# Fused attention, expert routing and two feed-forward layers: eight weight tiles are no longer decoded in the attention, and the decoder and the second route are laid out anew

## The chip, the cores and the metric

The kernel runs on one core of a Trainium2 chip. The metric is the device time of one execution in microseconds, the median of several runs. The engines are named as in the profile: PE (TensorE, matmuls; PEld its weight loads), DVE (VectorE), ACT (ScalarE), POOL (GpSimd), SP (SyncE, which here only issues DMAs).

## The reference

Three layers follow each other. The attention has no softmax: per head `kv = k^T v`, `out = q kv`, and each row of 64 is normalised by its root mean square. The 4608 tokens of width 512 are then routed to 8 experts with a greedy rule over all sorted logits, at most 576 tokens per expert, and each expert is a two-layer network with ReLU. The last layer takes the maximum of three products and one more product.

```
x      = norm(q @ (k.T @ v)) * g_norm                  # 8 batches x 576 tokens, 8 heads of 64
logits = x @ w_gate                                    # 4608 x 8
for idx in argsort(-logits.flatten()):                 # greedy
    tok, e = divmod(idx, 8)
    if assigned[tok] < 0 and counts[e] < 576: assigned[tok] = e
y[e]   = relu(x[e] @ w1[e]) @ w2[e]                    # 512 -> 1024 -> 512, per expert
out    = max(y @ v1, y @ v2, y @ v3) @ w_out           # 512 -> 768 -> 512
```

The four matrices of the last layer are 64-bit floats; all others are 32-bit.

## The kernel before, in words

**Attention** (the loop over `bp`, lines 437 to 488). Four passes of two batches each. A pass computes the K-V products (`kv`, line 189), copies them to SBUF on ScalarE (`kv_out`, 194 and 195), transposes them (`bd_t`, 200), multiplies in the gate weights (`bd_w`, 207), and then makes nine output tiles (`o_tile`, 225): ScalarE squares and copies each tile (230, 234), VectorE sums the squares (235), `norm_b` makes the norms and logits, and SP stores the rows (`y_store`, 271). K, V and Q of the next passes are loaded on SP (`load`), Q in two parts, the second ("r") when the tiles of the pass are done.

**Decoding.** The last layer's weights are 24 tiles of 128 x 512 numbers (0 to 17 of the three first matrices, 18 to 23 of the last). Each is loaded as 128 x 1024 32-bit words (`load64`, 355) and turned into an fp32 value and its split into two fp32r parts, in four steps: `dec_a`, two operations of ScalarE (367, 368); `dec_b`, a shift and a combination on VectorE (373, 375) and an addition on GpSimd (377); `dec_c`, a rounding copy on ScalarE (383, 385); `dec_d`, a subtraction (391, 394) on GpSimd for tiles 0 to 3 and 18 to 23, else on VectorE. Tiles 18 to 23 are stored to DRAM (395) and their buffers take tiles 12 to 17, which are loaded by `more64`. `TILES` says which tiles are decoded inside the attention, `ORDER` the sequence of the rest, and `decoder` is a generator that does one tile in two pieces.

**Threshold rounds** (`top_search`, 538). The first expert's threshold is found in seven rounds: VectorE compares all keys with up to 63 thresholds (573), TensorE counts (575), `narrow` compares the counts (542), TensorE spreads the result (545), VectorE sums it (548). Each round waits for the one before. `narrow` also begins a tile of the decoder (`begin`).

**Experts** (the loop over `p`, line 941). For each expert TensorE does both products of the expert and the last layer in groups of twelve matmuls (`mm3`, 880 to 882): three fp32r products for each fp32 one. After each group `tick` (906) runs one piece of the decoder and one step of `route`, the generator `phase(p + 1)` that finds the next expert's tokens. A route picks each token's best expert (`pick`, `keys`), transposes the masked keys on TensorE (708, 714, 717), and searches the threshold in 11 and 5 steps (`search`): two sign passes with a sum on ScalarE (506), a comparison on VectorE (508), a product (512), a matmul (515) and four small operations (519 to 526). Every `yield` is a tick between what stands before it and what stands behind. The rows of the next expert are then gathered (`gather`, 854), scaled (860) and transposed (869).

The order on each engine is the order of the program's text; a `yield` is what sets on which tick a step is issued. The lines that matter most:

```
    TILES = ((), (), (0, 1, 2, 3), (4, 5, 6, 7), ())
    ORDER = [8, 18, 9, 19, 10, 20, 11, 21, 22, 23] + list(range(12, 18))
        beat += 1
        bg_piece(1)
        if route is not None and beat > 6:
                next(route)
```

## Time and profile before

| what | value |
|---|---|
| median of 3 runs | 1289.95 us (1289.1 to 1290.58) |
| the profiled execution | 1291.93 us, its span 1290.2 us |
| busy share of the span: PE, PEld, DVE, ACT, POOL | 94%, 89%, 50%, 37%, 31% |
| the chain that ended last | PE 71%, DVE 13%, DMA 6%, ACT 5%, issue 3% |
| mean granted clock | 0.970 |
| HBM read and written | 111.43 MB, 23.20 MB |

The profile is of one execution. Busy time counts the time in which an engine has an instruction; a granted clock of 1.00 is 2.4 GHz, and an engine's idle time costs something only where the chain that ended last goes through it. The chain goes through the attention's loads to about 97 us, through the threshold rounds from 130 to 148, and then nearly always through TensorE.

### The profile page before, as it was taken

The numbers are of one execution on the slowest core, as the hardware profiler recorded it, in microseconds if no ns is written. First come the engines' busy times: TensorE is split into PE (matmuls) and PEld (weight loads), VectorE is DVE, ScalarE is ACT, GpSimd is POOL, SyncE is SP. The second block draws the span as 40 slices with busy tenths as digits, with TensorE's granted clock in tenths as the row PEclk, the third lists the DMA queues.
The fourth block names the chain that finished last, engine by engine and source line by source line (L and its number), as shares of the span: only waits on it lengthen the run. The fifth ranks groups of instructions, "written<-read, shape, count | busy, mean of one in ns | idle before, by whom it ended". The sixth has DMA issues, their size and how long they took to land.

```text
span 1290.2 us, 23274 instructions
## 1 busy us (share of the span) xinstructions
PE 1216.6 (94%) x8878; PEld 1142.4 (89%) x8880; DVE 645.4 (50%) x2075; ACT 480.8 (37%) x1166; POOL 401.9 (31%) x483
## 2 busy tenths in 40 slices
PE   9987687798999999999999999999999999999997
PEld 7876477798899989998999999998999899989995
DVE  2659779763576336652766157725763331122110
ACT  3557336641363225422552155314531331133110
POOL 0013025313531344134412452244313561154121
PEclk9979688899999999999999999999999999999998
DMA  9996534403230313121321133112302153013101
GB/s 337 403 362 230 199 96 162 156 1 102 90 101 18 104 42 110 63 84 45 107 75 58 48 114 99 58 47 95 105 28 83 58 157 103 1 57 115 66 1 41
DMA packets 52033, 136.15 MB, mean 106 GB/s; under 512 B 5840, under 2 KB 10448, under 8 KB 50384
## 3 DMA queue, kind: packets, MB, share of 16 engines
q1 hardware_dynamic: 44672, 110.25, 25.3%
q0 software_dynamic: 6944, 24.38, 5.6%
q8 instruction: 70, 1.15, 0.4%
q14 instruction: 43, 0.35, 0.1%
q10 hardware_dynamic: 304, 0.02, 0.0%
HBM read 111.43 MB, written 23.20 MB: 104 GB/s over the span
## 4 chain that ended last, share of the span: by engine, by line
PE 71%; DVE 13%; DMA 6%; ACT 5%; issue 3%; POOL 1%; SPq 1%; POOLq 0%; ACTq 0%; DVEq 0%
PE mm L880 18%; PE mm L882 17%; PE mm L881 17%; PE mm L1037 4%; PE mm L1039 4%; PE mm L1038 4%; ACT W L506 3%; DVE T L526 2%; DMA w<-w_dram 2%; PE kv L189 2%; DMA vta<-vx_dram 2%; PE tp L869 1%; DVE H L970 1%; PE o L225 1%; DMA xd<-y 1%
## 5 line engine op out<-in xcount | busy, mean ns | idle before, releaser
L880 PE MATMUL mm<-X,w 128*128 128x288 f32 x1152 | 345.7, 300 | 0.0
L882 PE MATMUL mm<-X,w 128*128 128x288 f32 x1152 | 340.3, 295 | 0.0
L881 PE MATMUL mm<-X,w 128*128 128x288 f32 x1152 | 340.3, 295 | 0.0
L880 PEld LDWEIGHTS mm<-X,w 128*128 128x128 f32 x1152 | 217.8, 189 | 0.4
L881 PEld LDWEIGHTS mm<-X,w 128*128 128x128 f32 x1152 | 217.4, 189 | 0.0
L882 PEld LDWEIGHTS mm<-X,w 128*128 128x128 f32 x1152 | 217.2, 189 | 0.0
L1012 POOL TENSOR_TENSOR H<-t,H 128x288 fp32r<-128x288 f32 x96 | 79.3, 826 | 432.7 <-ACT H L1011 432.7
L829 POOL TENSOR_TENSOR ring<-raw,ring 128x512 fp32r<-128x512 f32 x112 | 144.5, 1293 | 215.3 <-ACT ring L820 201.6
L1010 DVE TENSOR_TENSOR t<-mm,t 128x288 f32<-128x288 f32 x192 | 87.0, 453 | 164.7 <-PE mm L882 164.0
L880 PE MATMUL mm<-X,ring 128*128 128x288 f32 (+1 forms) x512 | 155.8, 304 | 1.6 <-ACT X L875 1.6
L880 PE MATMUL mm<-H,ring 128*128 128x288 f32 x512 | 156.0, 305 | 0.0
L882 PE MATMUL mm<-X,ring 128*128 128x288 f32 (+1 forms) x512 | 152.7, 298 | 0.3 <-DVE X L876 0.3
L881 PE MATMUL mm<-X,ring 128*128 128x288 f32 (+1 forms) x512 | 152.3, 298 | 0.0
L881 PE MATMUL mm<-H,ring 128*128 128x288 f32 x512 | 151.8, 296 | 0.0
L882 PE MATMUL mm<-H,ring 128*128 128x288 f32 x512 | 151.7, 296 | 0.0
L506 ACT ACTIVATE W<-KT,T 96x384 bf16<-96x384 f32 x168 | 102.1, 608 | 109.4 <-DVE T L526 109.4
L1011 ACT CAST H<-t 128x288 fp32r<-128x288 f32 x96 | 41.3, 430 | 262.9 <-DVE t L1010 262.9
L880 PEld LDWEIGHTS mm<-X,ring 128*128 128x128 f32 x512 | 98.2, 192 | 2.3 <-ACT X L875 2.3
L882 PEld LDWEIGHTS mm<-X,ring 128*128 128x128 f32 x512 | 97.6, 191 | 0.9 <-DVE X L876 0.9
L880 PEld LDWEIGHTS mm<-H,ring 128*128 128x128 f32 x512 | 97.4, 190 | 0.8 <-issue 0.8
L881 PEld LDWEIGHTS mm<-X,ring 128*128 128x128 f32 x512 | 97.8, 191 | 0.0
L881 PEld LDWEIGHTS mm<-H,ring 128*128 128x128 f32 x512 | 97.0, 190 | 0.0
(257 smaller groups left out, 2052.9 us busy)
## 6 DMA issues: line engine op xcount, KB each, us to landing
raw<-w_dram SPq DMA_DIRECT2D x128, 256.0 KB, 2.7
ring<-wod SPq DMA_DIRECT2D x48, 512.0 KB, 3.5
xd<-y SPq DMA_DIRECT2D x36, 288.0 KB, 8.5
w<-w_dram SPq DMA_DIRECT2D x18, 512.0 KB, 9.3
qta<-qx_dram SPq DMA_DIRECT2D x4, 1280.0 KB, 13.3
qtb<-qx_dram SPq DMA_DIRECT2D x4, 1024.0 KB, 11.1
kta<-kx_dram SPq DMA_DIRECT2D x3, 1280.0 KB, 17.5
vta<-vx_dram SPq DMA_DIRECT2D x3, 1280.0 KB, 16.6
```

The lines of the kernel that those rows point to most:

```text
L189: nc.tensor.matmul(KV[b][:, hp, :], KT[bp, o][p0:p1, c - o * CA, h], VT[bp, o][p0:p1, c - o * CA, h], start=(i == 0), stop=(i == len(cs) - 1))
L506: nc.scalar.activation(gs[:, j], KT, AF.Sign, bias=T[0:96, 1 + j:2 + j], scale=-1.0, accum_out=cnt[:, j:j + 1])
L829: (nc.gpsimd if stream[m][0] else nc.vector).tensor_sub(t[:, 1], raw, t[:, 0])
L880: nc.tensor.matmul(ps, wt[:, 0, ws], x[:, 0, xs], start=first, stop=False)
L881: nc.tensor.matmul(ps, wt[:, 1, ws], x[:, 0, xs], start=False, stop=False)
L882: nc.tensor.matmul(ps, wt[:, 0, ws], x[:, 1, xs], start=False, stop=last)
L1010: nc.vector.tensor_tensor(t2, ps[:, :HS], (t1, t1, t2)[j], op=OP.max)
L1011: nc.scalar.copy(m[:, 0, cs], t2)
L1012: nc.gpsimd.tensor_sub(m[:, 1, cs], t2, m[:, 0, cs])
L1037: nc.tensor.matmul(pss[c], l[:, 0, ls], w[:, 0, :], start=(fc == 0), stop=False)
L1038: nc.tensor.matmul(pss[c], l[:, 0, ls], w[:, 1, :], start=False, stop=False)
L1039: nc.tensor.matmul(pss[c], l[:, 1, ls], w[:, 0, :], start=False, stop=(fc == 5))
```

## The change

No tile is decoded in the attention (`TILES` is empty). Tiles 0 to 7 are loaded at the end of the third pass, behind the last load of Q, and the ten that were loaded at the end of the attention still are. `ORDER` begins with tiles 0 to 7. In the threshold rounds `narrow` begins two tiles, no longer one, and five of the rounds issue the shift of one tile on VectorE (`dec_x`), ahead of the comparison of the counts. In the expert loop the second route takes a step on every tick from the first, and the decoder a piece on every tick from the fifth. The routes have one more tick ahead of each transpose of masked keys (which the route of expert 1 had already), and the first eight search steps of expert 1's route have one more tick ahead of their matmul. A buffer for the shift's result is saved; `late` is replaced by the count of tiles that are ready.

```diff
--- before.py
+++ after.py
@@ -367,13 +367,16 @@
         nc.scalar.activation(up, up, AF.Copy, scale=2.0 ** -112)
         nc.scalar.activation(lo, lo.bitcast(U32), AF.Copy, scale=2.0 ** -29)
 
+    def dec_x(i):
+        XV[i] = w3a.tile([128, NH // 2 * XW], I32, name="dv", tag="xg", bufs=6)[:, 0:DM]
+        nc.vector.tensor_scalar(XV[i], words(i)[1], 3, None, op0=OP.logical_shift_left)
+
     def dec_b(i):
         r, up = words(i)
-        x = w3a.tile([128, DM], I32, name="dx", bufs=1)
-        nc.vector.tensor_scalar(x, up, 3, None, op0=OP.logical_shift_left)
-        yield
-        nc.vector.scalar_tensor_tensor(up, up, -2 ** 31, x, op0=OP.bitwise_and, op1=OP.bitwise_or)
-        XV[i] = w3a.tile([128, NH // 2 * XW], I32, name="dv", tag="xg", bufs=6)[:, 0:DM]
+        if i not in XV:
+            dec_x(i)
+        yield
+        nc.vector.scalar_tensor_tensor(up, up, -2 ** 31, XV[i], op0=OP.bitwise_and, op1=OP.bitwise_or)
         nc.gpsimd.tensor_tensor(XV[i], up, r, op=OP.add)
 
     def dec_c(i):
@@ -395,7 +398,7 @@
             nc.gpsimd.dma_start(wod[(i - 18) * 128:(i - 17) * 128], w.bitcast(F32).rearrange("p (j n) -> p j n", j=2))
             late64.append(i - 6)
 
-    ORDER = [8, 18, 9, 19, 10, 20, 11, 21, 22, 23] + list(range(12, 18))
+    ORDER = [0, 1, 2, 3, 4, 5, 6, 7, 8, 18, 9, 19, 10, 20, 11, 21, 22, 23] + list(range(12, 18))
     ND = len(ORDER)
     ready, late64, begun = [], [], []
 
@@ -433,7 +436,7 @@
             for _ in st_(i) or ():
                 pass
 
-    TILES = ((), (), (0, 1, 2, 3), (4, 5, 6, 7), ())
+    TILES = ((), (), (), (), ())
     for bp in range(NP):
         b0, b1, t0 = 2 * bp, 2 * bp + 1, bp * TP
         new = TILES[bp]
@@ -478,10 +481,13 @@
             y_store()
         if bp + 1 < NP:
             load(bp + 1, "r")
-        else:
+        if bp == NP - 2:
+            for i in range(0, NA):
+                load64(i)
+        if bp + 1 == NP:
             lds.close()
             w3p = ctx.enter_context(tc.tile_pool(name="w3p", bufs=1, side="right"))
-            for i in ORDER[:10]:
+            for i in ORDER[8:18]:
                 load64(i)
         norm_b()
         y_store()
@@ -495,7 +501,7 @@
     def bc(ap):
         return ap[:, :, None].to_broadcast([128, E, NT])
 
-    def search(KT, i0, i1, REM2):
+    def search(KT, i0, i1, REM2, slow):
 
         T = SC[:, i0]
         for i in range(i0, i1):
@@ -511,6 +517,8 @@
             ce = rt.tile([96, 3, E], BF, name="ce")
             nc.vector.tensor_mul(ce, BM, cnt[:, :, None].to_broadcast([96, 3, E]))
             yield
+            if slow and i < 8:
+                yield
             pc = rps.tile([128, 512], F32, name="rps")
             nc.tensor.matmul(pc[:, :3 * E], ones[0:96], ce.rearrange("p j e -> p (j e)"), start=True, stop=True)
             ex = rt.tile([128, 3, E], F32, name="ex")
@@ -538,9 +546,11 @@
     def top_search(g2):
 
         def narrow(pc, J, i, K):
+            if 2 <= len(begun) <= 10:
+                dec_x(ORDER[len(begun) // 2 - 1])
             ex = rt.tile([E, 64], BF, name="ex8")
             nc.vector.tensor_scalar(ex[:, 0:J], pc[0:E, 0:J], float(CAPN), None, op0=OP.is_gt)
-            begin(1)
+            begin(2)
             pb = rps.tile([128, 512], F32, name="rps")
             nc.tensor.matmul(pb[:, 0:J], ones8, ex[:, 0:J], start=True, stop=True)
             sc = rt.tile([128, 64], BF, name="scr")
@@ -707,8 +717,7 @@
                     gs = slice(12 * g, 12 * g + 12)
                     nc.vector.tensor_mul(K[:, g], oh[:, :, gs], key[:, None, gs].to_broadcast([128, E, 12]))
                 yield
-                if p == 1:
-                    yield
+                yield
                 pt = rps.tile([128, 512], F32, name="rps")
                 for g in range(3):
                     nc.tensor.transpose(pt[0:96, g * 128:g * 128 + 128], K[:, g].rearrange("p e c -> p (e c)"),
@@ -717,7 +726,7 @@
                 nc.scalar.copy(KT[i], pt[0:96, 0:384])
                 yield
             b1 = None
-            for r in search(KT[0], 0, 11, REM2):
+            for r in search(KT[0], 0, 11, REM2, p == 1):
                 if r is None:
                     yield
                 else:
@@ -734,7 +743,7 @@
             nc.vector.tensor_add(sf, sf, t)
             yield
             b2 = None
-            for r in search(KT[0], 11, 16, REM2):
+            for r in search(KT[0], 11, 16, REM2, False):
                 if r is None:
                     yield
                 else:
@@ -842,7 +851,6 @@
     X = xp.tile([128, 4, 2, S], F32R, name="X")
     LO = xp.tile([128, 6, 2, 128], F32R, name="LO")
     XG = {}
-    late = False
 
     def gather(p):
         for c in range(5):
@@ -906,13 +914,14 @@
     def tick():
         nonlocal route, beat
         beat += 1
-        bg_piece(1)
-        if route is not None and beat > 6:
+        if beat > 4:
+            bg_piece(1)
+        if route is not None:
             try:
                 next(route)
             except StopIteration:
                 route = None
-                if late:
+                if len(ready) == 24:
                     gather(len(XG) // 5)
 
     def drain():
@@ -1013,8 +1022,6 @@
             o = 64 * (p % 2)
             nc.gpsimd.tensor_copy(LO[:, fc, :, o:o + 64], m[:, :, 512:576].bitcast(F32))
         drain()
-        if p == 0:
-            late = True
         if (p + 1, 0) not in XG and p + 1 < E:
             gather(p + 1)
         if p + 1 < E:
```

Three places where the order of instructions moves. ScalarE, third pass of the attention, between the end of the second pass (L252) and the transposes' copy (L202); `w_0` and `w_1` are tiles 0 and 1:

```order
 L234 COPY y<-o 128x576
 L252 ACTIVATE t<-a 128x24
-L367 ACTIVATE w_0_549<-w_0_549 128x512
-L368 ACTIVATE w_0_549<-w_0_549 128x512
 L194 COPY BD_227<-kv 64x4x64
 L195 COPY BD_227<-kv 64x4x64
-L367 ACTIVATE w_1_551<-w_1_551 128x512
-L368 ACTIVATE w_1_551<-w_1_551 128x512
 L202 COPY bdt<-bt 128x512
 L208 COPY BD_227<-bt 128x4x16
```

The copies of the K-V product now follow the second pass directly; the first steps of tiles 0 and 1 are gone from there, and so are those of the other six.

VectorE, first threshold round (`W` is the comparison with the thresholds, `ex` that of the counts, `scr` the sum), before:

```order
L573 SCALAR_TENSOR_TENSOR W_1377<-H_232,ns,TH 128x372
L573 SCALAR_TENSOR_TENSOR W_1391<-H_232,ns,TH 128x372
L578 TENSOR_SCALAR H_232<-H_232,ns 128x36
L542 TENSOR_SCALAR ex_1406<-rps 8x31
L548 SCALAR_TENSOR_TENSOR scr,ns<-rps,SV 128x31
```

and of the change:

```order
L583 SCALAR_TENSOR_TENSOR W_1303<-H_232,ns,TH 128x372
L583 SCALAR_TENSOR_TENSOR W_1317<-H_232,ns,TH 128x372
L588 TENSOR_SCALAR H_232<-H_232,ns 128x36
L372 TENSOR_SCALAR dv<-w_0_947 128x512
L552 TENSOR_SCALAR ex_1334<-rps 8x31
L558 SCALAR_TENSOR_TENSOR scr,ns<-rps,SV 128x31
```

The shift of tile 0 stands between the subtraction and the comparison that waits for TensorE's counts; the next four rounds have the same.

SP, expert 0, behind the last weight loads of the first expert (`w_14` to `w_17` are the tiles loaded into freed buffers, `ring<-wod` the reads of the stored tiles 18 to 23), before:

```order
L355 DMA w_14_2385<-w_dram 128x1024
L355 DMA w_15_2501<-w_dram 128x1024
L355 DMA w_16_2563<-w_dram 128x1024
L817 DMA ring<-wod 128x1024
L355 DMA w_17_2619<-w_dram 128x1024
L817 DMA ring<-wod 128x1024 x3
```

and of the change:

```order
L355 DMA w_14_2967<-w_dram 128x1024
L355 DMA w_15_3019<-w_dram 128x1024
L355 DMA w_16_3080<-w_dram 128x1024
L355 DMA w_17_3135<-w_dram 128x1024
L826 DMA ring<-wod 128x1024 x4
```

The first read of the stored tiles now stands behind the last of the six loads.

## Rows read from the trace of the kernel before

**Rows 1.** Windows: us, busy (count) per engine, clock, DMA share, GB/s.

```profile
57.00:75.00 18.00, 12.79 (x98) 10.98 (x97) 10.45 (x38) 5.65 (x12) 0.62 (x3) 0.90 1.01 410
75.00:97.00 22.00, 20.77 (x136) 19.12 (x137) 12.57 (x25) 15.53 (x33) 4.60 (x5) 0.77 0.95 341
...
478.00:612.00 134.00, 132.50 (x976) 126.55 (x975) 73.71 (x258) 53.22 (x141) 48.03 (x55) 1.00 0.24 76
```

**Rows 2.** Timeline of the third pass: start, us, instruction [idle before <-releaser].

```profile
74.10 0.65 ACT L367 ACTIVATE w<-w 128x512 f32<-128x512 f32 x1 [9.59 <-DMA w<-w_dram]
...
75.99 1.12 PE L200 MATMUL bt<-ident,BD 128*128 128x128 f32 x4 [5.96 <-ACT BD L195]
...
76.69 0.55 SPq L107 DMA_DIRECT2D qtb<-qx_dram  x1
```

**Rows 3.** Windows of expert 0, engines PE, PEld, DVE, ACT, POOL.

```profile
175.00:190.00 15.00, 13.82 (x101) 13.47 (x101) 11.53 (x26) 6.64 (x15) 3.12 (x3) 1.00 0.20 54
190.00:240.00 50.00, 40.19 (x267) 38.78 (x266) 47.95 (x117) 32.32 (x75) 24.12 (x23) 0.90 0.48 164
240.00:264.00 24.00, 18.34 (x117) 17.54 (x116) 14.68 (x54) 11.48 (x32) 2.88 (x3) 0.86 0.24 89
264.00:312.00 48.00, 48.00 (x393) 46.96 (x392) 29.39 (x119) 14.46 (x41) 9.86 (x16) 1.00 0.12 39
```

**Rows 4.** Groups by line, 170 to 339 us: busy, mean ns | idle before, releaser.

```profile
L377 POOL TENSOR_TENSOR dv<-w 128x512 int32<-128x512 int32 x16 | 17.5, 1092 | 51.6 <-DVE w L375 26.8 <-DVE ce L512 8.8 <-ACT w L385 7.4
...
L375 DVE SCALAR_TENSOR_TENSOR w<-w,dx 128x512 int32<-128x512 int32 x16 | 12.0, 751 | 0.0
...
L373 DVE TENSOR_SCALAR dx<-w 128x512 int32<-128x512 int32 x16 | 9.7, 608 | 0.1
...
L391 DVE TENSOR_TENSOR w<-dv,w 128x512 fp32r<-128x512 f32 x10 | 8.2, 825 | 4.8 <-ACT w L383 4.7
...
L367 ACT ACTIVATE w<-w 128x512 f32<-128x512 f32 x9 | 6.1, 679 | 6.7 <-DMA w<-w_dram 6.7
```

**Rows 5.** Timeline of ScalarE: what it evacuates after ticks 13 and 38.

```profile
197.67 0.41 ACT L967 ACTIVATE H<-mm 128x288 fp32r<-128x288 f32 x1 [1.19 <-PE mm L882]
...
264.04 0.39 ACT L1007 COPY t<-mm 128x288 f32<-128x288 f32 x1
```

**Rows 6.** The chain that ended last: start, us, the fourth pass's transposes.

```profile
105.34 0.44 PE bt L200 x4
```

**Rows 7.** Timeline of ScalarE: last square of pass three with its copy, of pass four.

```profile
97.02 0.60 ACT L230 ACTIVATE sq<-o 128x512 f32<-128x512 f32 x1 [0.25 <-PE o L225]
97.52 0.63 ACT L234 COPY y<-o 128x576 f32<-128x576 f32 x1
...
122.75 0.60 ACT L230 ACTIVATE sq<-o 128x512 f32<-128x512 f32 x1 [0.47 <-PE o L225]
```

**Rows 8.** DMA issues, 76.5 to 77.5 us: count, KB each, us to landing.

```profile
qtb<-qx_dram SPq DMA_DIRECT2D x1, 1024.0 KB, 9.0
```

**Rows 9.** Timeline ahead of expert 0: gathers on GpSimd, the four subtractions on VectorE.

```profile
161.77 2.49 DVE L391 TENSOR_TENSOR w<-dv,w 128x512 fp32r<-128x512 f32 x4
...
162.58 1.32 POOL L854 DMA_INDIRECT xg<-xd,idx  x1 [0.31 <-issue]
164.20 0.95 POOL L854 DMA_INDIRECT xg<-xd,idx  x1 [0.30 <-issue]
```

**Rows 10.** Timeline of VectorE: a shift in the third pass, a comparison in the rounds.

```profile
74.79 0.43 DVE L373 TENSOR_SCALAR dx<-w 128x512 int32<-128x512 int32 x1 [5.80 <-ACT w L367]
...
133.58 0.18 DVE L542 TENSOR_SCALAR ex<-rps 8x31 bf16<-8x31 f32 x1 [0.29 <-PE rps L575]
```

**Rows 11.** Waits, whole span: us in total, times, longest.

```profile
ACT W L636 <- DVE q L634: 16.4, 2, 15.8
```

**Rows 12.** Waits of the key transposes: whole span, then 170 to 339 us.

```profile
PE rps L714 <- DVE V L708: 11.6, 6, 4.6
...
PE rps L714 <- DVE V L708: 4.6, 1, 4.6
```

## The prediction

> **What bounds the kernel now.** I read the chain that ended last first: TensorE holds most of it, so a change pays only where TensorE waits or runs slowly. The windows by stage then say where that is. In an expert of the steady state (478 to 612 us) TensorE is busy for 132.5 of 134 us at clock 1.00 [rows 1]: nothing to gain there but the 1.5 us. Two stages are not like that.
>
> The attention's third pass. ScalarE meets the first step of tile 0 at 64.5 us and stands 9.59 us until the tile's DMA has landed, at 74.1 [rows 2]. Behind it in ScalarE's queue stands the copy of the K-V product, and TensorE's transposes wait for that copy 5.96 us, to 75.99 [rows 2]. TensorE then runs at a mean clock of 0.77 for the next 22 us [rows 1], part of it at the lower of its two levels (1.2 GHz), which it entered with this hole. The DMA share is 1.01 and 0.95 in these two windows [rows 1]: the queues are full, the tiles are part of that load.
>
> Expert 0. VectorE is busy for 47.95 of the 50 us from 190 to 240, while TensorE is busy 40.19 at clock 0.90 [rows 3]; from 264 to 312 TensorE is continuous and VectorE busy 29.39 of 48 [rows 3]. So here VectorE is the bound for the first half and idle for much of the second. What ends the waits is the decoder and the second route at once on VectorE, and, at 240 to 264, ScalarE waiting for tiles that are loaded a second time: 6.7 us on DMA [rows 4].
>
> **Part by part.** A tick is one group of twelve matmuls and what is issued behind it; expert 0 has 67 of them, and the last 29 (264.04 to 312) take 48 us, 1.65 us each [rows 3, 5].
>
> *A, attention: no tile decoded, eight loads behind the last Q load.* The hole of 5.96 us goes, since ScalarE's copy no longer has a load ahead of it. The clock is worth a second term: from the transposes to the last square the third pass takes 75.99 to 97.02, 21.0 us, the fourth 105.34 to 122.75, 17.4 us [rows 2, 6, 7]; the difference, 3.6, is what a pass without the hole should not pay. Together 9.6; the fourth pass also loses its four first steps on ScalarE and the shifts on VectorE, some of which delay it. I take **-10**. What is late next is data: the second half of Q for this pass is issued at 76.69 and lands 9.0 us later, at 85.7 [rows 2, 8]. Four tiles of 0.524 MB ahead of it, at the 410 GB/s of that stage [rows 1], are 5.1 us, so it lands near 80.6. Without the hole the transposes start at 70.0. The last square follows 17.4 us later, at 87.4, and the four tiles that read this half cost ScalarE a square and a copy each, 0.60 + 0.63 us [rows 7], some 5 us: the half is wanted near 82.4, and just there. If data is the bound after all, the gain is those 5.1 us. Ends: -5 and -12. SP's queue is moved past nothing that is waited for: the eight loads stand behind the last Q load, and the stores of y behind them are first read by the gathers after 160 us [rows 9].
>
> *B, threshold rounds: 28 first-step operations on ScalarE, five shifts on VectorE.* ScalarE does 14 of them there now and then stands 15.8 us until VectorE's one-hot is made [rows 11]; fourteen more of 0.68 us [rows 4] are 9.5 us and fit. They cost nothing; without that cover a tile would cost its 1.4 us. The shifts stand ahead of a comparison before which VectorE is idle 0.29 us [rows 10], waiting for TensorE. A shift with GpSimd idle took 0.43 us [rows 10]. Five times 0.14 is 0.7, some of it covered by the shifts' overlap with the operation ahead: **+0.5**. Ends: 0, and five times 0.608 less 0.29, the mean of a shift in expert 0 [rows 4], where GpSimd works too: +1.6.
>
> *C, four subtractions leave VectorE before expert 0.* They run from 161.77 to 164.26; the gather that GpSimd writes beside them takes 1.32 us, a later one 0.95 [rows 9]. The scalings wait for gathers, so **-0.4**, ends 0 and -1. The Trainium skill (SBUF — State Buffer, section "Who interferes with whom") infers that a two-input VectorE operation does not hold up GpSimd's descriptor writing; by that sentence C would be 0. The rows speak for a little, and I follow them.
>
> *D, expert 0.* To VectorE's work come eight tiles of shift and combine, 8 x (0.608 + 0.751) = 10.9 us, less five shifts already done, 3.0, plus four subtractions of tiles 4 to 7, 4 x 0.825 = 3.3 [rows 4]: +11.1 on 103.6 us of busy time between 175 and 312 [rows 3], so 114.7. These operations' means include what GpSimd's extra adds cost. The idle time of VectorE there is now 33.4 us: 3.5 in the first window, 2.0, 9.3 and 18.6 [rows 3]. The route begins at tick 1, in the idle start; the decoder goes on to tick 55 instead of 35, with half of the search steps given three ticks, so that the idle tail shrinks from 29 ticks to 12 (7.7 of 18.6). Of the 9.3 I keep 6: the tiles loaded twice are again needed four ticks after their buffer is given back, but no read of the stored weights stands in SP's queue between them any more. With 1 at the start and 5 for new waits between ScalarE and VectorE, 20 us idle: 134.7 instead of 137, **-2**. Ends: idle 12 gives -10; idle as now gives +11.
>
> *E, later routes: one tick more ahead of the key transposes.* TensorE waits for the masked keys 11.6 us in six routes, 4.6 of it in expert 0, whose route has the extra tick already [rows 12]: 7.0 us in the five later ones, 1.4 each. A tick of 1.65 us covers nearly all: **-6**, ends -4 (if the search, two ticks later, meets worse places) and -7. The route ends two ticks later; its rows are gathered at its end, eight ticks before they are wanted.
>
> Sum: -10 + 0.5 - 0.4 - 2 - 6 = -17.9 on the profiled execution's 1291.93 us: 1274.0. That execution stands 2.0 us above the median of the runs shown (1289.95), so a median near 1272; I say **1273**.
>
> **Rivals.**
>
> *Data binds the attention* (0.15). A is -5 instead of -10: 1278. For it: DMA shares of 0.95 to 1.01 [rows 1]. Against: what the pass lacks is one transfer, and that moves up by as much as it is needed.
>
> *Expert 0 gains too* (0.15). VectorE idles only 12 us, D is -10: 1265. For it: VectorE did run 48 of 50 us without a gap when it had work [rows 3]. Against: a search step goes round ScalarE, VectorE and TensorE, and each of the three waits in it.
>
> *Expert 0 stretches, slower than before* (0.08). In the ticks with decoder and route together the pace was 197.67 to 264.04 for 25 ticks, 2.65 us [rows 5]; now 51 ticks have both. At that pace they take 135 us and the other sixteen 26: 161 instead of 137, +24, and the whole, with -2 replaced by +24, is 1273 + 26, about 1300. It decides from where D eats the other terms, +16: (137 + 16 - 26) / 51 = 2.5 us a tick. For it: every VectorE operation of the decoder gets company on GpSimd, where an add takes 1.09 us [rows 4]. Against: the slow stretch held the whole search at two ticks a step and 6.7 us of waits for loads. By the Trainium skill (SBUF — State Buffer, "Who interferes with whom") the port pair that VectorE shares with GpSimd is locked for a whole instruction. If every added GpSimd operation held VectorE in full, eight adds and four subtractions would be some 14 us and D near +12, an estimate by that page; the trace agrees that there is such a cost, since a shift takes 0.608 us there against 0.43 alone [rows 4, 10], but at 0.18 us a shift, not at 1.09.
>
> *The shifts wait for late tiles* (0.04). The change would not do what it says if tile 0 were not in place: VectorE would stand ahead of a comparison in every round. Against: the eight loads are 10.2 us at 410 GB/s [rows 1] and have the whole fourth pass, 25.7 us between last squares [rows 7]. A miss by 10 us would give 1283.
>
> **How the numbers follow.** The forecast itself has 0.58. What a measurement of this kernel can tell from no change is about 0.2%, 2.6 us. The forecast's own ends, A and D taken half way to theirs, are 1266 and 1282; the rivals widen that to **1261 to 1286**, which leaves out most of the slower case and the worst of the last. Faster 0.87, same 0.05 (D near +14 with the rest in place), slower 0.08.
>
> **What would show it.** Right: no idle time of ScalarE on a tile's DMA before 110 us; transposes of the third pass at 70 us; clock near 1.00 in the 20 us after; the threshold rounds ten us earlier and no longer than now by over 1 us; TensorE's wait for the masked keys near 5 us in all; the last group of expert 0 some 12 us earlier than 312. Wrong: TensorE waiting for Q in the third pass with VectorE and ScalarE idle (then A is data), a shift with idle time ahead of it in the rounds, or expert 0's groups taking over 150 us where they now take 137 (then D is the slower case).

## The result, and the profile after

The changed kernel takes **1277.6 us** (median of 3 runs, 1274.72 to 1278.84) against 1289.95: ratio 0.9901, 95% interval 0.9873 to 0.9928. The forecast was 1273, its range 1261 to 1286. The profiled execution of the change is the fastest of the three, 1274.72 us with a span of 1272.9; the prediction's sum for it was 1274.0. The total is close because errors of both signs met in it, and because of which execution was profiled: the sum was made for one 2.0 us above the median of its kernel, and is compared with one 2.9 us below the median of its own; median against forecast the miss is 4.6 us. Read by stage, from the starts of the same instructions in both timelines (the first comparison of counts in the threshold rounds, the second evacuation of expert 0, its last maximum on VectorE, the second evacuation of expert 1, the end of the span):

| stage, us | before | after | moved | predicted |
|---|---|---|---|---|
| start to the first comparison (A) | 130.45 | 118.93 | -11.5 | -10 |
| first to last comparison of the rounds (B) | 16.97 | 16.97 | 0.0 | +0.5 |
| from there to the second evacuation of expert 0 (C) | 31.17 | 28.74 | -2.4 | -0.4 |
| expert 0 to its last maximum (D) | 133.38 | 138.22 | +4.8 | -2 |
| gathers and output behind it | 29.05 | 27.84 | -1.2 | 0 |
| the other seven experts (E) | 949.2 | 942.2 | -7.0 | -6 |

The windows of the change by stage (us, busy and count of PE, PEld, DVE, ACT, POOL, clock, DMA share, GB/s), for [rows 1] and [rows 3]:

```profile
57.00:69.00 12.00, 11.76 (x92) 10.29 (x89) 9.77 (x35) 5.48 (x12) 0.61 (x3) 1.00 1.02 416
69.00:86.30 17.30, 16.73 (x140) 15.43 (x139) 7.51 (x17) 11.10 (x24) 0.20 (x1) 1.00 1.02 375
...
190.00:240.00 50.00, 38.91 (x263) 37.54 (x262) 43.71 (x107) 26.42 (x67) 21.21 (x20) 0.88 0.18 59
240.00:262.00 22.00, 17.86 (x118) 17.19 (x118) 20.01 (x54) 14.42 (x35) 14.59 (x17) 0.89 0.41 145
262.00:303.00 41.00, 36.66 (x291) 35.13 (x291) 29.78 (x101) 15.13 (x36) 11.06 (x15) 0.96 0.34 122
164.60:303.00 138.40, 118.83 (x860) 115.18 (x860) 116.28 (x318) 69.30 (x169) 55.45 (x57) 0.93 0.28 94
```

The third pass of the attention has no hole and the clock is 1.00 where it was 0.77. In expert 0 the pace is lost up to 262 and no longer made good behind: the last 41 us, where TensorE was continuous before, have 4.3 us of idle time and a clock of 0.96. The same stretch of the kernel before, first group to last, as one window:

```profile
178.60:312.00 133.40, 117.92 (x859) 114.68 (x858) 100.68 (x303) 64.02 (x159) 39.98 (x45) 0.94 0.28 97
```

VectorE is busy for 15.6 us more, the stage is 5 us longer. ScalarE's timeline of the change has, at the third pass, the copies of the K-V product that stood behind the tile, now waiting for TensorE's product and for no load, then the transposes' copy and the pass's last square; TensorE's has the transposes and its wait for the second half of Q; the DMA issues of 69.0 to 69.5 us have that half (count, KB, us to landing), for [rows 2], [rows 7] and [rows 8]:

```profile
66.78 0.36 ACT L194 COPY BD<-kv 64x256 f32<-64x256 f32 x1 [2.96 <-PE kv L189]
...
69.81 0.58 ACT L202 COPY bdt<-bt 128x512 f32<-128x512 f32 x1 [2.29 <-PE bt L200]
...
86.31 0.60 ACT L230 ACTIVATE sq<-o 128x512 f32<-128x512 f32 x1 [0.25 <-PE o L225]
```

```profile
69.17 0.60 PE L200 MATMUL bt<-ident,BD 128*128 128x128 f32 x4
...
80.97 1.22 PE L225 MATMUL o<-BD,qtb 128*128 128x144 f32 x8 [0.33 <-DMA qtb<-qx_dram]
```

```profile
qtb<-qx_dram SPq DMA_DIRECT2D x1, 1024.0 KB, 11.7
```

Issued at 69.09, it lands at 80.8 where it landed at 85.7; the last square of the pass follows at 86.31 instead of 97.02. The waits of the change over the whole span (us in total, times, longest), for [rows 12]: the wait for masked keys is 2.7 us where it was 11.6, the large one is now the wait of the search's matmul for the product it reads (`ce`, L518; L512 before).

```profile
PE rps L523 <- DVE ce L518: 18.7, 9, 5.5
...
PE rps L723 <- DVE V L718: 2.7, 3, 0.9
```

Before, in expert 0, that product was waited for 10.9 us in all, 8 times.

### The profile page after: what moved, and what is told of

The parts are those of the page before. It is cut to its first block, busy times and chain, and to the rows that moved or that the text cites. A ratio compares the mean times of both kernels' runs of the same rounds, so it can differ in the third digit from the quotient of the medians.

```text
span 1272.9 us, 23272 instructions
## 1 busy us (share of the span) xinstructions
PE 1208.8 (95%) x8878; PEld 1136.6 (89%) x8880; DVE 646.0 (51%) x2075; ACT 482.3 (38%) x1166; POOL 398.2 (31%) x483
## 4 chain that ended last, share of the span: by engine, by line
PE 77%; DVE 12%; ACT 5%; issue 2%; DMA 2%; POOL 1%; POOLq 0%; SPq 0%; ACTq 0%; DVEq 0%
PE mm L888 19%; PE mm L890 18%; PE mm L889 18%; PE mm L1044 4%; PE mm L1046 4%; PE mm L1045 4%; PE kv L189 4%; ACT W L512 3%; PE o L225 2%; DVE T L534 2%; PE tp L877 1%; DVE w L394 1%; DVE w L379 1%; DVE dv L372 1%; DMA vtb<-vx_dram 1%
## 5 line engine op out<-in xcount | busy, mean ns | idle before, releaser
L888 PE MATMUL mm<-X,ring 128*128 128x288 f32 (+1 forms) x512 | 153.7, 300 | 1.6 <-ACT X L883 1.6
L890 PE MATMUL mm<-X,ring 128*128 128x288 f32 (+1 forms) x512 | 151.1, 295 | 0.6 <-DVE X L884 0.6
L889 PE MATMUL mm<-X,ring 128*128 128x288 f32 (+1 forms) x512 | 150.7, 294 | 0.0
L512 ACT ACTIVATE W<-KT,T 96x384 bf16<-96x384 f32 x168 | 102.1, 608 | 117.3 <-DVE T L534 117.3
L888 PEld LDWEIGHTS mm<-X,ring 128*128 128x128 f32 x512 | 96.4, 188 | 2.2 <-ACT X L883 2.1
L888 PEld LDWEIGHTS mm<-H,ring 128*128 128x128 f32 x512 | 98.0, 191 | 0.0
L889 PEld LDWEIGHTS mm<-H,ring 128*128 128x128 f32 x512 | 97.5, 190 | 0.0
L890 PEld LDWEIGHTS mm<-H,ring 128*128 128x128 f32 x512 | 97.2, 190 | 0.0
L890 PEld LDWEIGHTS mm<-X,ring 128*128 128x128 f32 x512 | 96.1, 188 | 1.1 <-DVE X L884 1.1
```

The costliest lines, as they stand in the source:

```text
L512: nc.scalar.activation(gs[:, j], KT, AF.Sign, bias=T[0:96, 1 + j:2 + j], scale=-1.0, accum_out=cnt[:, j:j + 1])
L888: nc.tensor.matmul(ps, wt[:, 0, ws], x[:, 0, xs], start=first, stop=False)
L889: nc.tensor.matmul(ps, wt[:, 1, ws], x[:, 0, xs], start=False, stop=False)
L890: nc.tensor.matmul(ps, wt[:, 0, ws], x[:, 1, xs], start=False, stop=last)
```

## Experiments

Twelve kernels, each the change with one edit (the last three with two or three). Stages as in the table above, from the one profiled execution of each, so that a stage's length is a single reading (expert 0 takes 136.6 to 138.3 us in the five kernels that leave it as the change has it: the change, key tick undone, loads early, four subtractions, more idle matmuls); `ahead` is from the first comparison to the second evacuation of expert 0, `behind` the gathers and output behind it:

| kernel | median of runs, us | to first comparison | ahead | expert 0 | behind | rest | span |
|---|---|---|---|---|---|---|---|
| before | 1289.95 | 130.45 | 48.1 | 133.4 | 29.1 | 949.2 | 1290.2 |
| the change | 1277.6 | 118.93 | 45.7 | 138.2 | 27.8 | 942.2 | 1272.9 |
| key tick undone | 1285.9 | 119.12 | 48.3 | 138.3 | 27.8 | 951.0 | 1284.4 |
| loads early | 1282.86 | 125.18 | 47.1 | 137.5 | 28.7 | 942.2 | 1280.7 |
| tiles back | 1282.12 | 130.27 | 47.9 | 132.2 | 27.9 | 942.2 | 1280.4 |
| four subtractions | 1277.03 | 118.75 | 48.2 | 137.4 | 28.7 | 942.3 | 1275.4 |
| subtraction a tick later | 1275.83 | 118.88 | 48.3 | 137.1 | 27.9 | 941.9 | 1274.1 |
| subtractions on GpSimd | 1275.13 | 119.31 | 46.0 | 134.6 | 27.9 | 942.0 | 1269.7 |
| no tick in the steps | 1275.03 | 119.10 | 46.5 | 142.6 | 22.1 | 942.0 | 1272.3 |
| no shift in the rounds | 1277.66 | 118.49 | 48.4 | 138.2 | 28.6 | 942.3 | 1275.9 |
| more idle matmuls | 1276.18 | 119.42 | 47.4 | 136.6 | 29.0 | 942.3 | 1274.8 |
| all three, no tick | 1267.08 | 119.17 | 45.9 | 134.4 | 22.1 | 941.9 | 1263.5 |
| all three, four ticks | 1270.35 | 118.95 | 46.4 | 138.1 | 22.1 | 941.9 | 1267.5 |
| GpSimd, no tick | 1268.26 | 119.14 | 47.7 | 135.4 | 22.1 | 941.9 | 1266.3 |

**Key tick undone (E).**

```diff
                 yield
-                yield
+                if p == 1:
+                    yield
                 pt = rps.tile([128, 512], F32, name="rps")
```

> The change without its extra tick ahead of the key transposes in the routes after the first. Theory (the tick covers VectorE's masking): TensorE's wait for the masked keys goes from 2.7 us back to 7 us more, all of it after 330 us; attention, threshold rounds and expert 0 as with the change; time +7, about 1284.5. Rival (the later experts gained from elsewhere, as from an earlier route's place): the time moves by less than 3 us.

1285.9 us, ratio to before 0.9964 (0.9953 to 0.9975). All of the loss is in the last stage, and TensorE's wait is back; its waits over the whole span:

```profile
PE rps L724 <- DVE V L718: 7.1, 5, 1.8
```

E is what the prediction said: one tick for one wait. The rest is 8.8 us longer than with the tick and 7.0 was the difference of the two kernels; the extra is one expert that ran at a mean clock of 0.99 instead of 1.00 in this profile.

**Loads early (A: load or hole).**

```diff
-            for i in TILES[bp + 1]:
+            for i in ((), (0, 1, 2, 3), (4, 5, 6, 7))[bp]:
                 load64(i)
...
-        if bp == NP - 2:
-            for i in range(0, NA):
-                load64(i)
```

> The change with the eight tile loads back where they stood before (four behind the next pass's loads in passes two and three), still not decoded there. Theory (the hole came from ScalarE's queue, the loads cost little): transposes of the third pass stay near 69.5 us at clock 1.00, the second half of Q lands near 86 instead of 80.8, and only what it is then late for costs: +1 to +3.5 us at the first comparison of the rounds, time 1278.5 to 1281. Rival (data binds the attention): the whole 5.1 us of four tiles and more, +5 to +6. Other rival (loads are hidden altogether): 0.

1282.86 us, 0.9945 (0.9927 to 0.9963): +6.2 us at the first comparison, just above the rival's +5 to +6. The transposes still stand at 69.2. TensorE's timeline of the third pass, and the window behind:

```profile
85.72 1.54 PE L225 MATMUL o<-BD,qtb 128*128 128x144 f32 x5 [5.05 <-DMA qtb<-qx_dram]
```

```profile
87.00:93.00 6.00, 5.76 (x45) 5.17 (x44) 2.76 (x7) 3.85 (x8) 0.00 (x0) 0.83 1.02 409
```

With the hole gone and the loads in place TensorE waits 5.05 us for the second half of Q, which lands at 85.6, and then runs at 0.83. So the loads were not hidden: the last square of the pass comes at 92.55 here, at 86.31 in the change and at 97.02 before, so of the 10.7 us that the third pass lost they hold 6.2, with the hole gone, and the decoding with its hole the other 4.5.

**Tiles back (A and D).** Loads, `TILES` and `ORDER` as before, one tile begun a round, no shift there:

```diff
-    TILES = ((), (), (), (), ())
+    TILES = ((), (), (0, 1, 2, 3), (4, 5, 6, 7), ())
...
-            begin(2)
+            begin(1)
```

> The change with the eight tiles loaded and decoded in the attention again, and one tile begun in each threshold round; routes and decoder in the expert loop as changed. Theory (VectorE's work binds expert 0): the rounds begin near 130.5 again (+11.5), and expert 0, with eight tiles less on VectorE (about 15.6 us of it), takes 126 to 130 us instead of 138; time near 1281. Rival (the search's steps with their waits set the pace, not the work): expert 0 stays at 136 to 138, time near 1290.

1282.12 us, 0.9932 (0.9915 to 0.995). The rounds begin at 130.27. Expert 0 takes 132.2 us; window, and TensorE's two largest waits in it:

```profile
178.10:310.30 132.20, 116.82 (x859) 113.83 (x859) 102.68 (x302) 64.41 (x159) 41.07 (x45) 0.95 0.28 98
```

```profile
PE rps L520 <- DVE ce L515: 12.2, 4, 4.5
PE mm L883 <- ACT X L989: 2.4, 1, 2.4
```

This splits D: the new layout of route and decoder alone, with the same sixteen tiles, gains 1.2 us (133.4 to 132.2), which is less than like kernels differ by; the eight tiles cost 6.0 (to 138.2), which is more. They are 13.6 us of VectorE's busy time (102.68 to 116.28). So neither side of the expectation holds: VectorE's work counts, at less than half of its length.

**Four subtractions (C).**

```diff
+    scr = w3a.tile([128, NH // 2 * XW], F32, name="xg", bufs=6)[:, 0:DM]
+    for _ in range(4):
+        nc.vector.tensor_sub(scr, RING[0][:, 0].bitcast(F32), RING[0][:, 1].bitcast(F32))
     for c in range(2):
         scale(0, c)
```

> The change with four subtractions of 128x512 put on VectorE beside the first gathers, on other data, where four stood before. Theory (they hold up GpSimd's descriptor writing a little): the second gather takes 1.3 instead of 0.96 us, the first scaling comes 0.4 to 0.6 us later; if the first group of expert 0 then also meets TensorE at the lower clock, another 1.5 us: time +0.5 to +2.1. Rival (a two-input operation does not hold up descriptor writing, the gathers came earlier for another reason): the second gather stays at 0.95 and the time the same.

1277.03 us, 0.9893 (0.9876 to 0.9911): no cost that the runs show. Timelines of VectorE and of GpSimd in this kernel:

```profile
150.06 2.86 DVE L946 TENSOR_TENSOR xg<-ring 128x512 f32<-128x512 f32 x4
154.20 0.69 DVE L868 TENSOR_TENSOR xg<-xg 128x512 f32<-128x512 f32 x1 [1.28 <-DMA xg<-xd,idx]
156.10 0.69 DVE L868 TENSOR_TENSOR xg<-xg 128x512 f32<-128x512 f32 x1 [1.21 <-DMA xg<-xd,idx]
```

```profile
150.86 1.45 POOL L862 DMA_INDIRECT xg<-xd,idx  x1 [0.30 <-issue]
152.61 1.13 POOL L862 DMA_INDIRECT xg<-xd,idx  x1 [0.30 <-issue]
154.05 0.95 POOL L862 DMA_INDIRECT xg<-xd,idx  x1 [0.30 <-issue]
```

The second and third gather do take 1.45 and 1.13 us instead of 0.96 and 0.95. The first scaling waits only for the first gather, and comes at 154.20, no later than in the change (154.41). The second, which the first group of expert 0 needs too, waits for the second gather's data and comes at 156.10 instead of 155.38. So the profile leaves room for 0.7 us of cost or a little more, which the medians (1277.03 against 1277.6) do not show; the rest of the 2.5 us that this stage is longer here is mostly the lower clock of the first group, as below.

**Subtraction a tick later (D).**

```diff
-            if n >= 3:
-                dec_d(ORDER[n - 3])
             while len(begun) < min(ND, n + 2):
                 begin(1)
             if n < ND:
                 yield from dec_b(ORDER[n])
+            if n >= 3:
+                dec_d(ORDER[n - 3])
             yield
```

> The change with each tile's subtraction issued one tick later, behind the combination, so that it no longer stands directly behind ScalarE's rounding copy. Theory (VectorE is the bound of expert 0 up to about 275 us, so its waits count in full): its 9.1 us of waits for that copy go, and expert 0 gets 4 to 9 us shorter (129 to 134 instead of 138); time 1269 to 1274. Rival (the wait is only moved to the next step of the search): the wait goes and the time stays within 2 us.

1275.83 us, 0.9887 (0.9871 to 0.9904). VectorE's waits in expert 0:

```profile
DVE ce L518 <- ACT W L512: 9.1, 6, 4.4
...
DVE w L394 <- ACT w L386: 1.3, 1, 1.3
```

In the change the first was 2.2 us and the second 9.1: the wait has moved to the search, as the rival says, and expert 0 is 1.1 us shorter.

**Subtractions on GpSimd (D).**

```diff
-            (nc.gpsimd if i < 4 else nc.vector).tensor_sub(W3[i][:, 1], v, W3[i][:, 0])
+            nc.gpsimd.tensor_sub(W3[i][:, 1], v, W3[i][:, 0])
```

> The change with all subtractions of the decoder on GpSimd, fourteen of them off VectorE. Theory (VectorE's work binds expert 0, and GpSimd's operations stretch VectorE's by about a third of their own time, 18.4 us on 55.5 in the profile of the change): VectorE loses 14.1 us of work and 9.1 of waiting and gets about 7 of stretching from 21 us more of GpSimd; expert 0 6 to 10 us shorter, time 1268 to 1272. Rival (each GpSimd operation holds VectorE for its whole length): 14 operations of 1.5 us are 21 us, nothing is gained, time 1276 to 1280.

1275.13 us (1271.52 to 1279.29), 0.9889 (0.987 to 0.9909), by its runs alone not to be told from the change; expert 0 is 3.6 us shorter in the profile, which is of the fastest of its runs; neither side of the expectation holds. The window of expert 0, two of VectorE's groups in it (busy, mean ns | idle before), and TensorE's wait:

```profile
165.30:300.00 134.70, 114.87 (x860) 110.95 (x859) 120.96 (x304) 69.19 (x169) 76.31 (x71) 0.97 0.27 97
```

```profile
L372 DVE TENSOR_SCALAR dv<-w 128x512 int32<-128x512 int32 x19 | 18.1, 954 | 0.0
...
L534 DVE TENSOR_SCALAR T<-SC,T,tot 128x4 f32<-128x4 f32 x14 | 10.7, 761 | 0.5
```

```profile
PE rps L523 <- DVE ce L518: 17.8, 10, 5.0
```

Fourteen operations left VectorE, and it is busy for 4.7 us more (116.28 to 120.96): a shift now takes 0.954 us instead of 0.541, an operation on 128x4 numbers 0.761 instead of 0.474. TensorE's wait is nearly what it was. What is shorter is TensorE's own busy time, 118.83 to 114.87, at a clock of 0.97 instead of 0.93. VectorE's busy time is thus no measure of expert 0's length; why the clock was higher here no run shows.

**No tick in the steps (D).**

```diff
-            for r in search(KT[0], 0, 11, REM2, p == 1):
+            for r in search(KT[0], 0, 11, REM2, False):
```

> The change without the extra tick in the first eight search steps of the second route. Theory (VectorE's work sets the pace of expert 0, however many ticks a step is given): the ticks get longer while the route runs and shorter behind it, expert 0 stays within 2 us of 138, and with the route done eight ticks earlier the gathers come earlier and TensorE's wait of 4.0 us for the scaled rows shrinks: time 1273 to 1278. Rival (a step needs three ticks): TensorE's waits for the counts' product go from 18.7 to over 26 us and the time rises by 6 or more.

1275.03 us, 0.9881 (0.9864 to 0.9898). Windows of expert 0 and of the stage behind:

```profile
165.50:308.00 142.50, 118.96 (x860) 114.87 (x859) 114.41 (x317) 69.38 (x169) 59.14 (x62) 0.94 0.29 102
308.00:330.00 22.00, 22.00 (x118) 18.52 (x117) 5.82 (x9) 6.98 (x13) 10.86 (x11) 1.00 0.12 37
```

TensorE's waits in expert 0:

```profile
PE rps L523 <- DVE ce L518: 17.3, 12, 4.5
PE rps L615 <- DVE tots L607: 3.1, 1, 3.1
PE rps L656 <- DVE W L650: 2.3, 2, 1.3
```

Expert 0 is 4.4 us longer, the stage behind 5.7 shorter: TensorE has no idle time left there, since the gathers begin 12.3 us ahead of expert 0's end instead of 2.3 behind it. So expert 0 is not within 2 us of 138, as the theory had it, nor is the rival right: in the search TensorE waits 17.3 us, no more than the 18.7 with the tick. What is new are the waits of two later products of the route (L615 and L656), 5.4 us that the change does not have in expert 0. By their runs the two kernels cannot be told apart.

**No shift in the rounds (B).**

```diff
-            if 2 <= len(begun) <= 10:
-                dec_x(ORDER[len(begun) // 2 - 1])
```

> The change without the five shifts in the threshold rounds, which then are in expert 0 with the others. Theory (the rounds wait for TensorE where the shifts stand): the rounds take 17.0 us with or without them, within 0.2, and expert 0 gets 1 to 3 us longer for five shifts of 0.54 us: time +1 to +3. Rival (a shift in a round costs its 0.14 us beyond the idle time ahead): the rounds get 0.7 us shorter.

1277.66 us, 0.9901 (0.9885 to 0.9918): no difference, in the rounds (16.98 us) or in expert 0 (138.2). VectorE ahead of a comparison, in the change and then in this kernel:

```profile
121.68 0.42 DVE L372 TENSOR_SCALAR dv<-w 128x512 int32<-128x512 int32 x1
122.06 0.18 DVE L552 TENSOR_SCALAR ex<-rps 8x31 bf16<-8x31 f32 x1
```

```profile
121.62 0.18 DVE L550 TENSOR_SCALAR ex<-rps 8x31 bf16<-8x31 f32 x1 [0.29 <-PE rps L583]
```

The shift takes the place of the 0.29 us of idle time, and the comparison follows without a gap at the same distance from the round's start: its 0.42 us cost nothing, and leaving it out gains nothing. Five shifts in expert 0 are free too, against the theory's 1 to 3 us, which again says that VectorE's work there is partly covered.

**More idle matmuls (the 2.4 us ahead of expert 0).** From the first scaling to the second evacuation it took 10.1 to 10.2 us in three of the ten profiles so far, the change's own among them, and 11.4 to 12.8 in the others. What is added here are eight matmuls on zeros that feed nothing.

```diff
-            heat(18, hp)
+            heat(26, hp)
```

> The change with eight more idle matmuls (26 instead of 18) behind the indices of the first expert, so that TensorE is busy until the first gathered rows are scaled. Theory (the first group of expert 0 runs at 2.4 GHz where TensorE had little idle time before it, at 1.2 GHz where it had more): from the first scaling to the second evacuation it takes 10.2 to 10.8 us in the profile, as in three profiles so far, not 11.4 to 12.8, as in the other seven; time 1275 to 1276, runs closer together than 4 us. Rival (that spread comes from the gathers): the median stays at 1277.6 and the spread at 4 us. Third: the added matmuls delay the transposes by their 1.7 us, time 1278 to 1279.

1276.18 us (1275.62 to 1277.37), 0.9889 (0.9874 to 0.9904): within the runs of the change. The first group of expert 0 here, and then in the change and before:

```profile
158.70:161.80 3.10, 3.08 (x12) 2.79 (x13) 2.55 (x4) 0.48 (x1) 0.00 (x0) 0.50 0.00 0
```

```profile
157.50:159.70 2.20, 1.85 (x13) 1.65 (x14) 2.15 (x4) 0.52 (x2) 0.00 (x0) 1.00 0.20 82
```

```profile
170.20:173.30 3.10, 3.06 (x12) 2.78 (x13) 2.55 (x4) 0.49 (x1) 0.00 (x0) 0.50 0.05 21
```

The difference is the clock: 1.2 GHz against 2.4 in the same twelve matmuls. But TensorE had been busy until 0.75 us ahead of the transposes here, against 0.86 in the change, and ran the group at 1.2 all the same. Idle time just ahead does not decide it; the theory falls, and what does decide it stays open.

**All three, and two of them.** GpSimd's subtractions, no tick (`False`) or four (`i < 4`), 26 idle matmuls; the last kernel has 18.

> The change with all subtractions on GpSimd, no extra tick in the search steps, and eight more idle matmuls ahead of expert 0. Theory (the three act in different places and add up: -3.6 us in expert 0, -1.3 for expert 0 with the gathers behind it, -2 ahead of it): 1270 to 1272, below every kernel so far. Rival (GpSimd, busy for 78 of 135 us with the subtractions, delays the gathers and scalings that it also has to do): the stage between the last group of expert 0 and the first of the next goes back from 22 to 25 us or more, time 1274 or above.

> As the kernel with all three, but with the extra tick in the first four search steps instead of in none. Theory: the route ends four ticks later, early enough for the gathers (8 us ahead of the last group against 10 us of gathers and scalings), and TensorE's waits in the search are fewer: 1269 to 1272, within 2 us of the other. Rival (the extra tick pays in the steps, and the gathers' lead does not): 1267 to 1268.

> The change with all subtractions on GpSimd and no extra tick in the search steps, without the added idle matmuls. Theory (the two edits make the whole gain, the eight matmuls nothing): expert 0 takes 134 to 135 us as in the kernel with all three, the stage behind it 22 us, time within 2 us of its 1267.1. Rival (the matmuls keep the first group of expert 0 at 2.4 GHz in some executions): time 1268.5 to 1270.

Without the tick **1267.08 us** (1265.28 to 1269.6; 0.9821, 0.9808 to 0.9835), with four 1270.35 (0.9846, 0.9832 to 0.9859), without the added matmuls 1268.26 (0.9833, 0.9819 to 0.9846). Windows of the last, expert 0 and the stage behind:

```profile
166.80:302.30 135.50, 117.90 (x859) 113.76 (x859) 113.78 (x304) 69.35 (x169) 80.25 (x76) 0.95 0.30 107
302.30:324.40 22.10, 22.10 (x118) 18.67 (x117) 6.11 (x9) 6.99 (x14) 11.16 (x11) 1.00 0.11 37
```

By the medians the two edits do more than add up (1268.26, where each alone gives 1275): with the subtractions on GpSimd the search needs no extra tick (134.4 and 135.4 us without it, 134.6 with eight), and the 5.7 us behind expert 0 come free; GpSimd, busy for 80 of 135.5 us, does not delay the gathers. The matmuls add nothing that these runs show (the runs of the two kernels overlap). That expert 0 takes longer with four ticks (138.1 us) than with none or eight was foreseen by no theory. The 1270.35 lies in the theory's range, but not for its reason: TensorE's waits in the search are 17.3 us with four ticks and 14.0 without. Against the kernel with eight the waits are alike and TensorE's busy time differs, at a clock of 0.95 instead of 0.97; the cause stays open. Both kernels without the tick beat the change and the kernel before.

## Why the prediction was right, and where it was not

**A, attention: -11.5 for -10, right.** The third pass gained 10.7 (last square 97.02 to 86.31), the fourth 0.8. The transposes came at 69.2 for 70, the second half of Q landed at 80.8 for 80.6, and TensorE waited 0.3 us for it. The working held both parts, hole and load, and both are real: 4.5 and 6.2 us by the kernel with the loads early, while the tiles back restore both (130.27). The expectation for the early loads gave them at most 3.5; that was too little. The first rival (data binds) is wrong for the change, where the load moved up as the text said, but names what would have bound had only the hole been closed.

**B, rounds: 0.0 for +0.5.** At its lower end. ScalarE had the room that was counted, and no shift waited for a tile (the last rival): none of the five has idle time ahead of it.

**C, before expert 0: -2.4 for -0.4.** The step that failed is that a gather issued 0.4 us faster brings the scalings 0.4 us earlier, and that nothing else moves in this stage. The four subtractions do lengthen the second gather: 1.32, 1.32 and 1.45 us in the three kernels that have them, 0.95 to 0.97 in the other eleven. But the first scaling waits for the first gather, and the second waits for data that lands with more spread than that: it follows the first by 1.00, 0.86 and 1.90 us in those three, by 0.85 to 1.05 in ten of the others and by 1.58 in one. The Trainium skill (SBUF — State Buffer, section "Who interferes with whom") infers that a two-input VectorE operation does not hold up GpSimd's descriptor writing; by that there would be no hold-up at all. The gathers of 1.45 and 1.13 us beside four two-input operations, against 0.96 and 0.95, speak against that, though no run shows a cost in time. Of the -2.4, 0.7 lies ahead of the first scaling, within what that distance varies by over all kernels (18.5 to 19.5 us behind the last comparison), and 1.8 behind it, where the first group ran at a clock of 1.00 instead of 0.50 (2.2 us instead of 3.1) and the transposes beside it were faster too. That clock differs between nearly equal kernels; in eight of the twelve experiments the stage takes 47.1 to 48.4 us, as it did before. So the -2.4 is luck of the execution, and may be a good part of why it stands 2.9 us under the median.

**D, expert 0: +4.8 for -2, wrong in sign.** The step was: VectorE's work plus its idle time give the length, 114.7 + 20 = 134.7. Its busy time came to 116.3 and its idle time to 22.1, in a window 3.6 us shorter than the one used there, so work was under-sized by 4.5 (+15.6 for +11.1) and idle time by 2 to 3. The work was under-sized because the price of an operation was taken as fixed. VectorE's groups in expert 0 of the change:

```profile
L379 DVE SCALAR_TENSOR_TENSOR w<-w,dv 128x512 int32<-128x512 int32 x24 | 20.3, 847 | 0.0
L394 DVE TENSOR_TENSOR w<-dv,w 128x512 fp32r<-128x512 f32 x14 | 14.1, 1004 | 9.2 <-ACT w L386 9.1
...
L372 DVE TENSOR_SCALAR dv<-w 128x512 int32<-128x512 int32 x19 | 10.3, 541 | 0.0
...
L534 DVE TENSOR_SCALAR T<-SC,T,tot 128x4 f32<-128x4 f32 x14 | 6.6, 474 | 0.5
```

A combination takes 847 ns where it took 751 [rows 4], a subtraction 1004 where it took 825: at the old prices these 38 would be 29.6 us, and they are 34.4. The operation on 128x4 numbers, which no term held, went from 307 to 474 ns, 2.3 us in all. Not every price rose: a shift takes 541 where it took 608. One of the subtractions, VectorE and then GpSimd in the change:

```profile
231.68 2.73 DVE L394 TENSOR_TENSOR w<-dv,w 128x512 fp32r<-128x512 f32 x1 [1.32 <-ACT w L386]
```

```profile
231.45 0.58 POOL L398 DMA_DIRECT2D wod<-w  x1 [0.30 <-POOL w L397]
232.06 1.05 POOL L380 TENSOR_TENSOR dv<-w 128x512 int32<-128x512 int32 x1
233.06 0.80 POOL L1021 TENSOR_TENSOR H<-t,H 128x288 fp32r<-128x288 f32 x1
```

The subtraction, 0.69 us elsewhere, begins while GpSimd issues a store and ends 0.55 us behind the second of the two operations that follow there. By the Trainium skill (SBUF — State Buffer, section "Who interferes with whom") the shared port pair is locked for a whole instruction, and whoever issues first gets it. The trace agrees in that the subtraction outlasts both operations; the order it does not show, since by the profile VectorE started 0.38 us ahead of the addition and still ended behind it. The kernel with all subtractions on GpSimd fits too, where VectorE was busy longer (120.96 us) with fourteen operations less. But with the search's extra tick gone as well it was busy for 113.3 and 113.8 us, with as much on GpSimd: how the operations meet counts, and not only how many there are.

But the sum's form was also wrong. The length of expert 0 is TensorE's busy time and its waits, and VectorE's work enters through both: 117.92 busy and 15.5 of waits before, 118.83 and 19.4 after. So of the +4.8, 3.9 is waits: those for the search's product grew from 10.9 to 18.7, one for masked keys (4.6) went, and 0.7 for another product came. The other 0.9 is busy time, at a clock of 0.93 instead of 0.94. Where it was lost ScalarE's evacuations after ticks 13 and 38 show, here in the change, for [rows 5]:

```profile
184.38 0.41 ACT L976 ACTIVATE H<-mm 128x288 fp32r<-128x288 f32 x1 [0.24 <-PE mm L890]
```

```profile
242.12 0.39 ACT L1016 COPY t<-mm 128x288 f32<-128x288 f32 x1
```

From tick 13 to tick 38, the stretch that was slow before, the change takes 57.7 us instead of 66.4; from there to the last maximum 60.7 instead of 47.9. The idle tail took up work, as the sum had it, but not for nothing: TensorE, which had no idle time there, now waits.

Eight tiles of 13.6 us cost 6.0; five shifts cost nothing; with fourteen subtractions moved off, and a VectorE busier than before, the stage was 3.6 shorter in the fastest run of that kernel, all in the clock. Of the two rivals on D, "gains too" had the sign wrong. "Stretches" had the sign right and the size wrong: over the 51 ticks with both decoder and route, from 171.00 to 284.92 by the same evacuations, a tick took 2.23 us, not 2.65. The stage's last group came 9 us earlier than before, at 303, not 12.

**Behind expert 0: -1.2 for nothing,** not examined further by a kernel of its own; the stage varies by as much (27.8 to 29.1 us) over kernels that are alike in it. The prediction also missed what lay there to be had: 5.7 us once the route ends early.

**E, later routes: -7.0 for -6, right,** at its far end. One wait of 1.4 us an expert, covered by one tick.

The total was right because A, C and the stage behind gave 4.7 us more than predicted, E 1.0 and B 0.5, and D took 6.8. A and E are the mechanism as predicted; that C and the stage behind made up for half of D's miss is luck.

## What to carry to other kernels

Price an operation that shares something with another engine from the stage as it will be, not as it is: the mean of a row holds the company that the engine had. Where two causes of one delay lie in the same place (a queue's wait and a late transfer), closing one uncovers the other, so put one back alone to see what it holds. An extra tick that is to hide a wait also moves whatever comes at the end of that chain; look what waits there before it is spent.

## What was not expected of the hardware

- VectorE's small operations are stretched beside GpSimd too: the one on 128x4 numbers takes 0.29 us in some places and 1.41 in one (at 248.68, in the change, until GpSimd's operations of 247.81 to 250.06 are over), and 0.761 on the mean with all subtractions on GpSimd. That is 0.47 more, where a shift of 128x512 took 0.53 more than its 0.42.
- GpSimd's issue of an indirect gather took 1.45 us beside a row of two-input subtractions on VectorE, 0.95 without.
- TensorE's clock in one and the same group of twelve matmuls was 0.50 in some profiles and 1.00 in others of nearly equal kernels, worth 0.9 us in the group and 1.2 or more from the first scaling to the second evacuation. With 26 idle matmuls ahead and 0.75 us of idle time it was 0.50; with 18 and 0.86 us it was 1.00.
